# A gated linear recurrence followed by routed experts: a list-scheduled program graph, a one-hot inverse permutation and one evacuation for q and k

## The chip, the cores and the metric

One core of one Trainium2 chip. The time is device microseconds of one execution; a kernel is executed several times and the median is given, with the lowest and highest. Each execution has a state: slow if it took over 1.5% more than the fastest one of the same kernel in the same round of runs, else fast; ratios use fast runs alone. The runs fell on several chips; where a chip is named, it is by the number that the runs record (0, 9 and 15; the chip of the first pair of kernels is not recorded).

Words for the engines: PE is TensorE (PEld its weight loads), DVE is VectorE, ACT is ScalarE, POOL is GpSimd, SP is SyncE, which here only starts transfers.

## The reference

```python
# q, k, v, a_re, a_im: [4, 8, 768, 48];  x: 3072 rows of 384;  8 experts, 384 -> 1024 -> 384
mag = sqrt(a_re**2 + a_im**2); scale = minimum(mag, .999) / (mag + 1e-6)
ar, ai = a_re * scale, a_im * scale
for t in range(768):                                  # per batch and head
    S_re, S_im = ar*S_re - ai*S_im + k[t] v[t]^T, ar*S_im + ai*S_re
    y[t] = q[t] @ S_re
x = rows of y, heads side by side                     # 3072 x 384
for e in range(8):
    m = domain_id == e
    out[m] = relu(x[m] @ w1[e]) @ w2[e]
```

Both kernels run the recurrence in tiles of 256 positions of a batch: 12 tiles ("groups"), each with a preparation (logarithms and angles, running sums by matmul, exponentials, sines) and four **steps**, one per pair of heads: transposes of k and q, scores, a causal mask, outputs. There are 48 steps. The rows of a finished batch are gathered per expert, put through two layers and scattered to the output: 4 x 8 = 32 **expert runs** of 128 rows each.

## The kernel before

Its order is hand-made: `prep` gives eight portions of a group's preparation, spread over the steps of the group before; an expert runs where `plan` says; the weights of expert e are loaded in five parts at steps 1 + 5e on. The inverse permutation (which row goes to which expert slot) is made by 24 scatters to memory and read back:

```python
    def scatter_inverse(b):
        for c in range(6):
            col = b * 6 + c
            unordered(f"inv{b}", nc.gpsimd.indirect_dma_start(
                out=inv_ap[b][:, :],
                out_offset=bass.IndirectOffsetOnAxis(ap=dest_i[:, col:col + 1], axis=0),
                in_=tok_i[:, col // 2, col % 2, :], in_offset=None))

    def load_inverse(b):
        nc.sync.dma_start(out=inv_sb[b][:, :, :], in_=inv_ap[b][0:NMAIN, :].rearrange("(p e) two -> p e two", e=NE))
    # ... in the loop over steps:
            if s == 2:
                for b in range(B):
                    scatter_inverse(b)
                    load_inverse(b)
```

The transposed q and k leave PSUM in two copies, q in turn on ACT and DVE, k always on DVE into a buffer with zeros between its halves:

```python
        if s % 2 == 0:
            nc.scalar.copy(out=qt[...], in_=t_ps[0:96, 0]...)          # cut
        else:
            nc.vector.tensor_copy(out=qt[...], in_=t_ps[0:96, 0]...)   # cut
        nc.vector.tensor_copy(out=kt[...][:, :, 0:3:2, :], in_=t_ps[0:96, 1]...)   # cut
```

The experts' PSUM buffers are one of each kind (`x` for transposes and second layer, `wh` for the first layer), shared with the steps.

Of the kernel before, what the change touches and what calls it, by code (L numbers as in the profile page):

```python
# [29 lines left out]
NE = 8  # L30
# [8 lines left out]
GROUPS = [[0], [1], [2, 3], [4, 5], [6, 7], [8, 9], [10, 11]]  # L39
SET_LE = "natural_log_exp_and_others"  # L40
SET_TRIG = "trig_and_small"


@with_exitstack
def kernel(
# [14 lines left out]

    nosync = mybir.DependencyInfo(mybir.DependencyClass.NoSync, mybir.DependencyReason.DATA)

    def after(ins, prev):
        if prev is not None:
            tc.add_manual_dep(ins.ins, prev.ins.name, nosync, reason="order")
        return ins

    last = {}

    def chain(key, ins):  # L70
        after(ins, last.get(key))
        last[key] = ins
        return ins
# [24 lines left out]
    def src_view(t, g):  # L98
        b, i = divmod(g, NT)
        return t[b, :, i * TS:(i + 1) * TS, :].rearrange("h (p j) d -> p h (j d)", j=2)  # L100

    loaded = {}

    def load(g, names):
        for name, t in names:
            bufs = {"ar": 2, "ai": 2, "q": 2, "k": 2, "v": 2}[name]
            tl = lpool.tile([128, H, 96], F32, name=f"ld_{name}", tag=f"ld_{name}", bufs=bufs)
            nc.sync.dma_start(out=tl[:, :, :], in_=src_view(t, g))
            loaded[name, g] = tl

    ARI = [("ar", a_re), ("ai", a_im)]
    QKV = [("k", k), ("q", q), ("v", v)]
    load(0, ARI)


# [6 lines left out]
    mask = cpool.tile([128, 2, 2, 2, CP], BF16, name="mask")  # L122
    for c in range(2):
        r = slice(c * CP, (c + 1) * CP)
        for js in range(2):
            for jt in range(2):
                u = (u_str if js > jt else u_inc)
                for hh in range(2):
                    nc.vector.tensor_copy(out=mask[r, hh, js, jt, :], in_=u[r, r])
    VB, CB = 2, 2  # L130
    vz = [cpool.tile([128, H, 2, 3, D], BF16, name=f"vz{n}") for n in range(VB)]
    cz = [cpool.tile([96, 2, 2, 3 * CP], BF16, name=f"cz{n}") for n in range(CB)]
# [3 lines left out]
    for t in cz:  # L136
        nc.vector.memset(t[:, :, :, CP:2 * CP], 0.0)
    ident = cpool.tile([128, 128], BF16, name="ident")
    make_identity(nc, ident[:, :])
    ident16 = cpool.tile([128, 128], F16, name="ident16")  # L140
# [8 lines left out]


    dest_i = cpool.tile([128, NCOL], I32, name="dest_i")
    ovf_i = cpool.tile([1, 1], I32, name="ovf_i")
    tok_i = cpool.tile([128, B * NT, 2, 2], I32, name="tok_i")
    inv_sb = [cpool.tile([128, NE, 2], I32, name=f"inv_sb{b}") for b in range(B)]
    XSLOTS = 5
    xrow = [cpool.tile([128, HD], F16, name=f"xrow{n}") for n in range(XSLOTS)]
    for t in xrow:
        nc.gpsimd.memset(t[:, :], 0.0)

    def routing():  # L160
        rpool = mpool
        e8 = rpool.tile([128, 8], F32, name="e8", bufs=1)
        nc.gpsimd.iota(e8[:, :], pattern=[[1, 8]], base=0, channel_multiplier=0,
                       allow_small_or_imprecise_dtypes=True)
        nc.gpsimd.iota(tok_i[:, :, :, 0], pattern=[[TS, B * NT], [1, 2]], base=0, channel_multiplier=2)
        for c in range(2):
            nc.gpsimd.iota(tok_i[c * CP:(c + 1) * CP, :, :, 1].rearrange("p (b i) j -> p b i j", b=B),
                           pattern=[[0, B], [TS, NT], [128, 2]], base=c, channel_multiplier=2)
        sent = rpool.tile([128, NROWS // 64], I32, name="sent", tag="xt", bufs=2)
        nc.gpsimd.iota(sent[:, :], pattern=[[1, NROWS // 64]], base=OOB_SENT, channel_multiplier=NROWS // 64)  # L170
        for b in range(B):
            nc.scalar.dma_start(out=inv_ap[b][:, :].rearrange("(p c) two -> p (c two)", p=128), in_=sent[:, :])

        dom_i = rpool.tile([128, B * NT, 4], I32, name="dom_i", tag="xt", bufs=2)
        h32 = dataclasses.replace(moe_domain_id.tensor, shape=[NTOK * 2], dtype=I32)
        nc.scalar.dma_start(out=dom_i[:, :, :],
                            in_=bass.AP(tensor=h32, offset=0, ap=[[4, 128], [TS * 2, B * NT], [1, 4]]))
        fb = rpool.tile([128, 4, NCOL], F32, name="fb", tag="o_sb", bufs=2)
        rank, main, over = fb[:, 1], fb[:, 2], fb[:, 3]
        domf = fb[:, 0].rearrange("p (c j) -> p c j", j=2)  # L180
        nc.vector.tensor_copy(out=domf[:, :, :], in_=dom_i[:, :, 0:4:2])
        dcol = domf[:, :, :].rearrange("p c j -> p (c j)")
        oh = rpool.tile([128, NCOL, 8], F16, name="oh", tag="xst", bufs=2)
        nc.vector.tensor_tensor(out=oh[:, :, :], in0=e8[:, None, :].to_broadcast([128, NCOL, 8]),
                                in1=dcol[:, :, None].to_broadcast([128, NCOL, 8]), op=ALU.is_equal)
        r_ps = big("r_ps")
        nc.tensor.matmul(out=r_ps[:, 0, 0:NCOL * 8], lhsT=u_str[:, :], rhs=oh[:, :, :], start=True, stop=True)
        nc.tensor.matmul(out=r_ps[:, 1, 0:NCOL * 8], lhsT=ones16[:, :], rhs=oh[:, :, :], start=True, stop=True)
        cr = rpool.tile([128, 2, B, 6, 8], F32, name="cr", tag="h_sb", bufs=2)
        cnt, rk = cr[:, 0], cr[:, 1]  # L190
        nc.vector.tensor_copy(out=cnt[:, :, :, :], in_=r_ps[:, 1, 0:NCOL * 8])
        nc.vector.tensor_copy(out=rk[:, :, :, :], in_=r_ps[:, 0, 0:NCOL * 8])
        for c in range(1, 6):
            nc.vector.tensor_tensor(out=rk[:, :, c, :], in0=rk[:, :, c, :], in1=cnt[:, :, c - 1, :], op=ALU.add)
            nc.vector.tensor_tensor(out=cnt[:, :, c, :], in0=cnt[:, :, c, :], in1=cnt[:, :, c - 1, :], op=ALU.add)
        ovf = rpool.tile([1, 1], F32, name="ovf", bufs=1)
        nc.vector.tensor_reduce(out=ovf[:, :], in_=cnt[0:1, :, 5, :], axis=AX.XY, op=ALU.max)
        nc.vector.tensor_copy(out=ovf_i[:, :], in_=ovf[:, :])
        rk3 = rk[:, :, :, :].rearrange("p b c e -> p (b c) e")
        nc.vector.tensor_tensor(out=rk3, in0=rk3, in1=oh[:, :, :], op=ALU.mult)  # L200
        nc.vector.tensor_reduce(out=rank[:, :], in_=rk3, axis=AX.X, op=ALU.add)
        nc.vector.scalar_tensor_tensor(out=main[:, :], in0=rank[:, :], scalar=float(NE), in1=dcol,
                                       op0=ALU.mult, op1=ALU.add)
        nc.vector.scalar_tensor_tensor(out=over[:, :], in0=dcol, scalar=float(OVC * 128), in1=rank[:, :],
                                       op0=ALU.mult, op1=ALU.add)
        nc.vector.scalar_tensor_tensor(out=over[:, :], in0=over[:, :], scalar=float(NMAIN - CAP), in1=main[:, :],
                                       op0=ALU.add, op1=ALU.subtract)
        nc.vector.tensor_scalar(out=rank[:, :], in0=rank[:, :], scalar1=float(CAP), scalar2=None, op0=ALU.is_ge)
        nc.vector.tensor_tensor(out=over[:, :], in0=over[:, :], in1=rank[:, :], op=ALU.mult)
        nc.vector.tensor_tensor(out=main[:, :], in0=main[:, :], in1=over[:, :], op=ALU.add)  # L210
        nc.vector.tensor_copy(out=dest_i[:, :], in_=main[:, :])

    def scatter_inverse(b):
        for c in range(6):
            col = b * 6 + c
            unordered(f"inv{b}", nc.gpsimd.indirect_dma_start(  # L216
                out=inv_ap[b][:, :],
                out_offset=bass.IndirectOffsetOnAxis(ap=dest_i[:, col:col + 1], axis=0),
                in_=tok_i[:, col // 2, col % 2, :], in_offset=None))

    def load_inverse(b):
        nc.sync.dma_start(out=inv_sb[b][:, :, :], in_=inv_ap[b][0:NMAIN, :].rearrange("(p e) two -> p e two", e=NE))
# [5 lines left out]
    def load_weights(e, part, gate):  # L228
        if part < 3:
            i = nc.gpsimd.dma_start(out=w1t[e][:, part, :], in_=moe_w1[e, part * 128:(part + 1) * 128, :])  # L230
        else:
            j = (part - 3) * 4
            i = nc.gpsimd.dma_start(out=w2t[e][:, j:j + 4, :],
                                    in_=moe_w2[e, j * 128:(j + 4) * 128, :].rearrange("(j p) f -> p j f", p=128))
        tc.add_manual_dep(i.ins, gate.ins.name, syncdep, reason="inputs first")


    lm = {}
    th = {}
    ep = {}  # L240
    em = {}
    sc = {}

    def flat(t):
        return t[:, :, :].rearrange("p h x -> p (h x)")

    def jhd(ap):
        return ap.rearrange("p h (j d) -> p j h d", j=2)

    def hdx(ap):  # L250
        return ap.rearrange("p j (h d) -> p j h d", h=H)
# [384 lines left out]
```

## Time and profile before

| what | before | from |
|---|---|---|
| time, median of the runs with the profile | 355.4 us (349.9 to 355.8) | timed runs |
| span of the profiled execution (taken apart from these four) | 342.6 us | page |
| masks of step 0 / 4 / 26 / 47 | 28.4 / 63.1 / 178.4 / 285.1 us | timeline, `mtm` on DVE |
| expert runs done by step 26 / 47 | 4 / 21 | timeline, `h_sb` |
| last matmul | 331.9 us | timeline |

By the rule above three of these four runs (355.4 to 355.8) count as slow and only 349.9 as fast.

The masks are used as milestones throughout: each step has exactly one. The page's first part gives busy time, share of the span and number of instructions of each engine:

```profile
PE 235.1 (69%) x2642; PEld 178.5 (52%) x2642; DVE 186.3 (54%) x356; ACT 184.0 (54%) x246; POOL 162.2 (47%) x188
```

No engine is near full over the whole span. The slices, the stages and the scatters are shown in the prediction. In the list of waits (total us, times, longest), three of those that end with something the profile calls "remote", that is, a release it can't put to any engine or transfer of this core:

```profile
DVE mtm L405 <- remote: 11.0, 2, 6.1
DVE fg L312 <- remote: 6.9, 1, 6.9
ACT h_sb L462 <- remote: 6.7, 1, 6.7
```

All waits of this kind sum to 38.1 us over the engines (some run at the same time). One of the two on `mtm` and the one on `fg` lie at 37 to 43 and 46 to 53 us.

### The profile page before, as it was taken

The numbers are of one execution on the slowest core, as the hardware profiler recorded it, in microseconds if no ns is written. First come the engines' busy times: TensorE is split into PE (matmuls) and PEld (weight loads), VectorE is DVE, ScalarE is ACT, GpSimd is POOL, SyncE is SP. The second block draws the span as 40 slices with busy tenths as digits, with TensorE's granted clock in tenths as the row PEclk, the third lists the DMA queues.
The fourth block names the chain that finished last, engine by engine and source line by source line (L and its number), as shares of the span: only waits on it lengthen the run. The fifth ranks groups of instructions, "written<-read, shape, count | busy, mean of one in ns | idle before, by whom it ended". The sixth has DMA issues, their size and how long they took to land.

```text
span 342.6 us, 6624 instructions
## 1 busy us (share of the span) xinstructions
PE 235.1 (69%) x2642; PEld 178.5 (52%) x2642; DVE 186.3 (54%) x356; ACT 184.0 (54%) x246; POOL 162.2 (47%) x188
## 2 busy tenths in 40 slices
PE   0247432854567758967685798997899799729960
PEld 0026211731255536755473676785688688527740
DVE  4684236574787659676973878666963241000100
ACT  4545404555287236886593677878563554313540
POOL 5227776162024444453347835535885432752230
PEclk9999555675588679989996999999999999987996
DMA  8970075899929979979979699576547112120110
GB/s 195 234 149 1 7 119 81 186 212 239 274 43 151 232 170 163 189 139 267 246 124 199 165 188 265 140 113 104 121 77 150 59 60 81 57 61 21 54 57 21
DMA packets 83126, 46.40 MB, mean 135 GB/s; under 512 B 68273, under 2 KB 78479, under 8 KB 83088
## 3 DMA queue, kind: packets, MB, share of 16 engines
q1 hardware_dynamic: 64704, 25.99, 32.5%
q0 software_dynamic: 16256, 19.70, 31.6%
q10 hardware_dynamic: 2128, 0.22, 0.5%
q8 instruction: 22, 0.36, 0.5%
q14 instruction: 16, 0.13, 0.2%
HBM read 51.96 MB, written 8.87 MB: 178 GB/s over the span
## 4 chain that ended last, share of the span: by engine, by line
PE 23%; issue 17%; ACT 17%; DVE 13%; DMA 13%; POOL 12%; another core or an unknown queue 1%; POOLq 0%; SPq 0%; DVEq 0%; ACTq 0%
POOL gl_inv_rows L216 6%; PE h_ps L459 5%; PE o_ps L469 5%; PE cum L264 5%; DMA xrow<-gl_x_rows,inv_sb 3%; ACT L479 3%; DMA gl_x_rows<-xst 3%; DMA ld_v<-in_v_dram 3%; POOL out_dram L472 3%; PE t_ps L381 2%; DVE fg L312 2%; PE mt L402 2%; ACT la L272 2%; POOL xrow L441 2%; DMA gl_inv_rows<-tok_i,dest_i 2%
## 5 line engine op out<-in xcount | busy, mean ns | idle before, releaser
L405 DVE TENSOR_TENSOR mtm<-mt,mask 128x512 bf16<-128x512 f32 x48 | 33.0, 687 | 47.9 <-PE mt L402 35.2
L459 PE MATMUL h_ps<-xt,w1t 128*128 128x128 f16 x768 | 51.1, 222 | 6.7 <-ACT h_sb L462 6.7
L472 POOL DMA_INDIRECT out_dram<-o_sb,inv_sb x32 | 33.3, 1040 | 46.9 <-ACT o_sb L471 42.1
L462 ACT ACTIVATE h_sb<-h_ps 128x1024 f16<-128x1024 f32 x32 | 32.7, 1021 | 38.5 <-PE h_ps L459 28.0
L459 PEld LDWEIGHTS <-w1t 128*128 128x128 f16 x768 | 46.6, 100 | 9.3 <-issue 7.6
L469 PE MATMUL o_ps<-w2t,h_sb 128*128 128x384 f16 x256 | 49.5, 336 | 2.1 <-DVE xt L451 1.0
L441 POOL DMA_INDIRECT xrow<-gl_x_rows,inv_sb x32 | 37.1, 1160 | 17.0 <-issue 6.9
L402 PE MATMUL mt<-qt,cz 96*128 96x128 bf16 x384 | 34.2, 237 | 7.7 <-DVE cz L391 6.9
L451 DVE COPY xt<-xt_ps 128x384 f16<-128x384 f16 x32 | 11.3, 352 | 45.0 <-PE xt_ps L449 35.9
L402 PEld LDWEIGHTS <-cz 96*128 96x128 bf16 x384 | 27.4, 107 | 16.0 <-DVE cz L391 10.1
L469 PEld LDWEIGHTS <-h_sb 128*128 128x128 f16 x256 | 24.5, 101 | 16.4 <-issue 3.8
L216 POOL DMA_INDIRECT gl_inv_rows<-tok_i,dest_i x24 | 24.8, 1033 | 16.7 <-DVE fg L315 9.7
L348 POOL CAST vz<-ld_v 64x768 bf16<-64x768 f32 x24 | 24.5, 1020 | 13.3 <-issue 5.1
L421 PE MATMUL y<-vz,mtm 128*128 128x96 bf16 x192 | 20.0, 216 | 15.1 <-DVE mtm L405 9.8
L346 POOL CAST vz<-ld_v 128x768 bf16<-128x768 f32 x12 | 11.8, 980 | 37.1 <-issue 15.4
L318 ACT ACTIVATE sc<-fg 128x768 bf16<-128x768 f32 x12 | 10.1, 843 | 34.0 <-DVE fg L313 24.5
L292 ACT ACTIVATE em<-cum,bias_m 128x768 bf16<-128x768 f32 x12 | 10.8, 897 | 27.1 <-PE cum L264 22.4
L264 PE MATMUL cum<-lm,u_inc 128*128 128x384 f16 x36 | 12.9, 419 | 16.5 <-DVE lm L283 16.5
L230 POOL DMA_DIRECT2D w1t<-in_moe_w_dram x24 | 14.3, 595 | 20.7 <-DVE mtm L405 20.3
L391 DVE COPY cz<-t_ps 96x512 bf16<-96x512 bf16 x48 | 19.8, 412 | 5.8 <-ACT qt L386 4.9
L421 PEld LDWEIGHTS <-mtm 128*128 128x128 bf16 x192 | 13.1, 100 | 18.6 <-DVE mtm L405 12.9
L264 PEld LDWEIGHTS <-ones 128*128 128x128 f16 x96 | 10.3, 116 | 23.5 <-issue 15.6
(90 smaller groups left out, 522.2 us busy)
## 6 DMA issues: line engine op xcount, KB each, us to landing
w1t<-in_moe_w_dram POOLq DMA_DIRECT2D x24, 256.0 KB
w2t<-in_moe_w_dram POOLq DMA_DIRECT2D x16, 384.0 KB
ld_ar<-in_a_re_dram SPq DMA_DIRECT2D x12, 384.0 KB
ld_ai<-in_a_im_dram SPq DMA_DIRECT2D x12, 384.0 KB
ld_k<-in_k_dram SPq DMA_DIRECT2D x12, 384.0 KB
ld_q<-in_q_dram SPq DMA_DIRECT2D x12, 384.0 KB
ld_v<-in_v_dram SPq DMA_DIRECT2D x12, 384.0 KB
gl_x_rows<-xst SPq DMA_DIRECT2D x12, 192.0 KB
```

Of the source, the lines that this page charges most:

```text
L216: unordered(f"inv{b}", nc.gpsimd.indirect_dma_start(out=inv_ap[b][:, :], out_offset=bass.IndirectOffsetOnAxis(ap=dest_i[:, col:col + 1], a ...
L264: chain("pe_cum", nc.tensor.matmul(out=o, lhsT=l[:, :], rhs=r, start=(n == 0), stop=(n == len(mm) - 1)))
L348: nc.gpsimd.tensor_copy(out=vt[c * CP:(c + 1) * CP, :, :, 1 + c, :], in_=vsrc[c * CP:(c + 1) * CP])
L391: nc.vector.tensor_copy(out=kt[:, :, :, :].rearrange("p h j (c t) -> p (h j) c t", c=3)[:, :, 0:3:2, :], in_=t_ps[0:96, 1].rearrange("p h ...
L402: nc.tensor.matmul(out=mt[:, hh, js, :], lhsT=kt[:, hh, js, c * CP:(c + 2) * CP], rhs=qt[:, hh, c, :], start=(c == 0), stop=(c == 1))
L405: m = nc.vector.tensor_tensor(out=mtm[:, :, :, :].rearrange("p a b t -> p (a b t)"), in0=mt[:, :, :, :].rearrange("p a b t -> p (a b t)"), ...
L421: chain("pe_y", nc.tensor.matmul(out=o, lhsT=mtms[s][:, hh, js, :], rhs=vz[g % VB][:, pr * 2 + hh, js, 1:3, :], start=(js == 0), stop=False))
L441: nc.gpsimd.indirect_dma_start(out=x[:, :], out_offset=None, in_=x_ap[b][:, :], in_offset=bass.IndirectOffsetOnAxis(ap=idx, axis=0), bound ...
L459: nc.tensor.matmul(out=h_ps[:, j // 4, (j % 4) * 128:(j % 4 + 1) * 128], lhsT=w1[:, fs, j * 128:(j + 1) * 128], rhs=xt[:, fs, :], start=(f ...
L462: nc.scalar.activation(out=h_sb[:, :, :].rearrange("p j t -> p (j t)"), in_=h_ps[:, :, :].rearrange("p a t -> p (a t)"), func=AF.Relu)
L469: nc.tensor.matmul(out=o_ps[:, :], lhsT=h_sb[:, j, :], rhs=w2[:, j, :], start=(j == 0), stop=(j == 7))
L472: ins = nc.gpsimd.indirect_dma_start(out=out[:, :], out_offset=bass.IndirectOffsetOnAxis(ap=inv, axis=0), in_=o_sb[:, :], in_offset=None, ...
```

## The change

The whole program becomes a graph of some thousand pieces with modelled costs. At build time a list scheduler places each piece, in order of earliest start, on one of the engines allowed for it, and the resulting order is frozen. Beside that: the inverse permutation is computed on chip by one-hot matmuls; k and q leave PSUM in one copy (k transposed with its halves swapped, so that both fit one pattern); the first group is prepared in two halves; value masks are cut from the bf16 tile; weights are spaced for the last part to start at step 26; in the last batch the experts alternate between two PSUM buffers.

```diff
+def order(ops, rings):                       # cut to its core
+    while cand:
+        # for each ready piece: the engine on which it would end first, and its start there
+        t0, e0 = min((x[0], x[1]) for x in best)
+        t, e, c, o = min((x for x in best if x[1] == e0 and x[0] <= t0 + SLACK), key=lambda x: (x[3].pos, x[0]))
+        o.start, o.on = t, e
+        # ... engine, DMA and ring times move on; successors become ready
...
-    def scatter_inverse(b): ...
-    def load_inverse(b): ...
+    def rt_r(b, e):                            # six selections of a batch, on POOL or DVE
+        for c in range(6):
+            (nc.gpsimd if e == "POOL" else nc.vector).tensor_scalar(
+                out=T["R", b][:, c, :], in0=slots[:, :], scalar1=rank[:, b * 6 + c:b * 6 + c + 1], scalar2=None, op0=ALU.is_equal)
+        # ... V = one-hot of the expert times (row, row in batch, 1)
+    def rt_q(b):
+        for c in range(6):
+            nc.tensor.matmul(out=T["I", b][:, :, :], lhsT=T["R", b][:, c, :], rhs=T["V", b][:, c], start=(c == 0), stop=(c == 5))
...
+    def out_kq(s, slot, e):
+        cp(e, kq[slot][:, 0:8 * 3 * CP].rearrange("p (b x) -> p b x", x=3 * CP)[:, :, CP:],
+           tps[s][0:96].rearrange("p k h c t -> p (k h c) t"))
...
+            xr, xi, ti, hi, he, oi, ob = (Inst("xrow"), Inst("tm" if last and e % 2 else "x"), Inst("xt"),
+                                          Inst("cum" if last and e % 2 else "wh"), Inst("h_sb"),
+                                          Inst("tm" if last else "x"), Inst("o_sb"))
```

## The prediction

> **What bounds the kernel now.** I read the page's slices first, then the stages by window, the groups, and the waits.
>
> ```profile
> PE   0247432854567758967685798997899799729960
> DVE  4684236574787659676973878666963241000100
> ACT  4545404555287236886593677878563554313540
> PEclk9999555675588679989996999999999999987996
> DMA  8970075899929979979979699576547112120110
> ```
>
> No engine is full throughout. TensorE (PE) is full only from about slice 25 on; DMA is full from slice 7 to 24; DVE and ACT are half full everywhere. So I cut the span at the masks of steps (48 steps, one `mtm` each; step 0 at 28.4 us, step 4 at 63.1, step 26 at 178.4, step 47 at 285.1):
>
> ```profile
> 0.00:27.30 27.30, 6.57 (x36) 3.53 (x36) 16.89 (x62) 13.31 (x15) 10.18 (x30) 1.00 0.88 181
> 27.30:62.00 34.70, 16.81 (x124) 11.55 (x124) 15.18 (x23) 12.77 (x17) 25.84 (x27) 0.62 0.34 55
> 62.00:116.60 54.60, 34.11 (x295) 23.14 (x296) 38.30 (x57) 30.04 (x40) 15.75 (x20) 0.69 0.95 190
> 116.60:200.00 83.40, 62.83 (x720) 47.80 (x718) 60.02 (x103) 55.88 (x75) 42.10 (x44) 0.89 0.92 191
> 200.00:289.00 89.00, 81.12 (x1123) 67.35 (x1122) 52.65 (x102) 56.29 (x81) 48.16 (x48) 1.00 0.57 119
> 289.00:333.50 44.50, 33.61 (x351) 25.09 (x348) 3.22 (x9) 15.67 (x22) 19.86 (x20) 0.92 0.17 56
> ```
>
> Columns: length, then busy PE, weight loads, DVE, ACT, POOL, then PE clock, DMA share, GB/s. Five regimes: a serial prologue; 34.7 us in which only POOL works (25.84) and DMA falls to 0.34; 138 us with DMA at 0.92 to 0.95 and DVE and ACT near 70%; 89 us with PE at 81.12 of 89; a tail with PE at 75%.
>
> Why the second stage is empty is in the waits of the SP queue:
>
> ```profile
> SPq L222 <- DMA gl_inv_rows<-tok_i,dest_i: 32.1, 5, 12.2
> ```
>
> (in total, times, longest), and in the groups (busy, mean ns, then idle before with its releasers):
>
> ```profile
> L216 POOL DMA_INDIRECT gl_inv_rows<-tok_i,dest_i x24 | 24.8, 1033 | 16.7 <-DVE fg L315 9.7
> L391 DVE COPY cz<-t_ps 96x512 bf16<-96x512 bf16 x48 | 19.8, 412 | 5.8 <-ACT qt L386 4.9
> L386 ACT COPY qt<-t_ps 96x512 bf16<-96x512 bf16 x24 | 13.9, 578 | 6.2 <-PE t_ps L381 5.9
> L348 POOL CAST vz<-ld_v 64x768 bf16<-64x768 f32 x24 | 24.5, 1020 | 13.3 <-issue 5.1
> L469 PE MATMUL o_ps<-w2t,h_sb 128*128 128x384 f16 x256 | 49.5, 336 | 2.1 <-DVE xt L451 1.0 <-ACT o_sb L471 0.6 <-ACT h_sb L462 0.5
> ```
>
> The 24 scatters of the inverse permutation hold POOL from 23.0 to 56.0 us, and the SP queue, in order, holds the next groups' loads behind reading that inverse back. The chain of waits goes through exactly this (scatters, then a read-back landing, then `ld_v` from 61.7 for 6.6 us).
>
> **What the Trainium skill says.** "VectorE: DVE Perf Modes", section "Why PSUM operands drop a tier": a PSUM operand allows at most the packed 16-bit mode. The trace agrees: 512 bf16 elements in 412 ns is 267 ns of streaming at two per cycle of 0.96 GHz plus 145 fixed. "PSUM — Partial Sum Buffer", section "The four PSUM rules": POOL cannot touch PSUM; so freed POOL time can only take SBUF pieces (here `values`, `vmask`, selections), none of the evacuations. "DMA: Bandwidth & Descriptors", Specifications: transfers under 512 B are below line rate; 68273 of the 83126 packets are that small, and a 0.95 share moves only 190 GB/s. "TensorE: Matmul & The Clock Gate", Part 1: an idle window of about 3.4 us halves the clock; the trace agrees: after 5.4 us idle at 301 us, one expert's first layer took 2.72 us instead of 1.50.
>
> **The change part by part.**
> - Inverse permutation. Removed: 24 scatters x 1.033 = 24.8 us of POOL, four fills, four read-backs, and 20-odd small DVE operations. Added: per batch seven small selection operations on DVE or POOL, six small matmuls, three small DVE operations: some 2 us a batch (an estimate from the 0.17 to 0.36 us of the small routing operations). None of it is needed before step 12. What it frees is the second stage. The next group's preparation is seven ACT operations of 0.84 to 0.93, two exponentials of 0.9 and two table loads of 1.28, 10.4 us, with some 10 us of DVE interleaved; so step 4 can come 16 to 18 us after step 0 rather than 34.7: about -17 us.
> - First group in two halves, routing behind it. Now DVE does routing while `em` and `th` wait (13.1 to 21.9 us), and ACT and DVE alternate on full tiles. Halves pipeline, at more fixed cost: about -5 us.
> - One evacuation for q and k. 1024 elements by the rate above: 533 + 145 = 0.68 us on DVE, 48 x 0.68 = 32.6 us. It replaces 48 x 0.412 + 24 x 0.412 on DVE (29.7) and 13.9 on ACT. Sum -11 us of engine time, and one semaphore hop less per step; the 6.9 us that scores waited for `cz` are all the path can gain from that.
> - Value masks from the bf16 tile, on DVE or POOL. POOL's 24.5 us of 64-row casts become about 0.72 us per group on DVE (12 groups, 8.6 us, an estimate from a 768-element cast at the fastest mode plus fixed time) or twice the POOL time of now. POOL was no bound after 62 us, so this is near zero.
> - Placement by earliest finish. DVE + ACT now total 186 + 184 = 370 us; the change leaves about 367. Both can be near 184, while PE needs, at full clock from the chain's pieces, 48 steps x 1.26 (0.45 scores, 0.45 transposes, 0.36 outputs), 12 x 1.05 state, 32 of running sums (192 matmuls of 384 columns at 0.165, six in 0.99) and 32 experts x 2.81 (1.34 + 1.30 + 0.17): 60 + 13 + 32 + 90 = 195 us. DMA's two big queues take 32.5% + 31.6% of 342.6 = 220 us. Four resources near 190 to 220 us: the end is set by how well they overlap.
> - Weights earlier: the last part at step 26 instead of 40. By step 26 DMA did 0.88x27.3 + 0.34x34.7 + 0.95x54.6 + 0.92x61.8 = 145 us of work; 14 more weight parts of about 1.75 us (an estimate: 70 us of the 108 on the software queue over 40 parts) make 168.
> - Tail: hidden and output PSUM tiles alternate between two buffers for the last batch. An expert now takes 3.07 us (each `out_dram` 3.07 apart, 312.7 to 328.0) and can take PE's 2.81: 8 x 0.26 = 2 us. Experts of batch 2 filling the wait of about 5.4 us from the last x store to the first gathered row (289.2 to 294.6): about 4 us more.
>
> **The sum.** Step 0 at 22, step 4 at 39. Step 26: from the engines (DVE + ACT, about 113 us each by then, at 75% use) 150; from DMA, 168/0.95 = 177. I take 165, since no engine waits for loads for long in 62 to 200 now (`vz` waited 13.6 us for `ld_v`, most of it at the start) and weights may land late. After it: 22 steps at 1.95 us of PE (running sums and states included) is 43, and 25 experts x 2.81 is 70: 113 us, against 78% use before (331.9 - 178.4 = 153 us for 120); I give the new order 93%: 121 us. Then 10.7 from the last matmul to the end, as now (331.9 to 342.6). 165 + 121 + 11 = 297 for a profiled execution. The timed median lies 3.7% above the profile now (355.4 against 342.6), some of it luck in the stalls: four stalls of 4.8 to 6.9 us (38 to 43, 47 to 53, 263 to 268, 301 to 306) where engines wait for something the profile calls remote or issue. I add 1%: **300 us**.
>
> **Rivals.**
> 1. DMA takes the place of the scatters. For it: share 0.95 already, and the change asks for 25 us more by step 26. Single-buffered q, k, v loads leave less slack. Then step 26 stays at 177 or later, and the end is 310 to 330.
> 2. The list order is frozen from modelled costs. Queues are strictly in order, so a piece whose inputs are late blocks those behind it; waits move from PE to elsewhere. For it: clocks of 0.62 to 0.69 early, which a fixed matmul cost ignores, and stalls of 5 us. Against: the order now is hand-made and frozen too, at 78%. If use stays near 80%, the end is 318.
> 3. Everything overlaps as planned: DMA's 220 us less the tail's share packed before the last 35 us gives a floor near 255; 270 to 280 if engines hold 90% from the start.
> 4. Nothing or worse, if a new queue (POOL with gathers behind weight gates) blocks the experts: needs all of 55 us to be eaten; unlikely.
>
> **Range and chances.** 276 (rival 3) to 330 (1 and 2 together, plus stalls). Faster than 348 us needs only the second stage's 17 us and something of the rest: 0.92. Within 2%: 0.05. Slower: 0.03.
>
> **What would show it.** Right: no scatters or read-back; step 0 near 22 and step 4 near 39 us; a single evacuation of 96x1024 near 0.68 us; DVE and ACT each near 184 us; PE above 90% after step 26; last experts 2.8 us apart. Wrong: DMA share under 0.85 between steps 4 and 26 with engines still idle (the order, not DMA, is the bound), long waits of POOL for masks with PE idle behind gathers, or PE waiting on evacuations after step 26.

## The result, and the profile after

The changed kernel takes **307.5 us** (305.1 to 310.5), the kernel before 355.4 in the same runs: ratio 0.872, 95% interval 0.857 to 0.887. A ratio here is the mean time of one kernel's fast runs over that of the other's of the same rounds, profiled executions left out, so not quite the ratio of the medians quoted. This first one can't be recomputed exactly from the runs listed: 306.7 over the one fast run of 349.9 would be 0.877. The profiled execution took 310.5 us and counts as slow; the kernel was profiled again later in a fast execution (span 305.3), whose milestones are the same within 3.5 us.

The slices of the changed kernel (span 308.7 us, a slice is 7.7 us):

```profile
PE   1335738457687899167498689899889999877960
DVE  4969878858999897047979669897579444100100
ACT  3667578838869984027697549675765344434430
PEclk9999988956999999769799879999999999999997
DMA  7998599999999999978989523517321021112110
```

DVE is fuller in the first half than before (8 and 9 where 5 to 7 stood), the hollow of the scatters is gone from all lines, and DMA is done with its bulk at slice 22 rather than 31. The same as stages, cut at the masks and where the picture changes (columns: length; busy PE, weight loads, DVE, ACT, POOL; PE clock, DMA share, GB/s):

```profile
0.00:32.80 32.80, 11.47 (x117) 8.90 (x118) 24.76 (x89) 19.06 (x30) 15.81 (x41) 1.00 0.95 205
32.80:49.20 16.40, 10.36 (x115) 8.03 (x115) 13.16 (x23) 13.03 (x15) 3.94 (x6) 0.90 0.97 178
94.30:111.00 16.70, 14.26 (x197) 11.61 (x198) 15.07 (x27) 14.99 (x20) 11.84 (x14) 1.00 1.19 253
111.00:133.00 22.00, 13.02 (x191) 11.01 (x189) 11.13 (x18) 7.58 (x12) 9.19 (x11) 0.86 1.13 234
200.00:258.90 58.90, 55.48 (x760) 45.57 (x759) 41.18 (x72) 32.72 (x44) 22.25 (x21) 1.00 0.27 76
258.90:300.00 41.10, 33.87 (x402) 25.75 (x399) 3.69 (x11) 17.36 (x24) 19.40 (x20) 1.00 0.18 57
```

Row 1 is the prologue: it got longer, 32.8 us. Row 2: the first four steps take 16.4 us instead of 34.7. Rows 3 and 4: the DMA share is over 1, and in row 4 the engines are half idle all the same. Row 5: PE at 94%.

| milestone | before | predicted | after |
|---|---|---|---|
| step 0 | 28.4 | 22 | 32.8 |
| step 4 | 63.1 | 39 | 49.2 |
| step 26 | 178.4 | 165 | 163.6 |
| step 47 | 285.1 | | 258.2 |
| last matmul | 331.9 | 286 | 298.9 |
| span | 342.6 | 297 | 308.7 |

The total came out 2.5% above the predicted 300. On the way three stretches were off by over 10 us, not all in one direction (to step 0, steps 4 to 26, and after step 26), so the experiments go at the parts.

Two views bear on the prologue, and a third is used later. First, the chain of waits from 7 to 19 us (start, length, what), in which two blocks of selections on POOL stand in the path:

```profile
8.62 0.36 DVE rank L479
...
9.08 4.79 POOL sel L484 x6
...
13.92 0.21 PE iv_ps L493
...
14.29 4.00 POOL sel L484 x6
```

Then the durations of the selections by engine, from the answer for the tile `sel` (minimum/median/maximum in ns, first and last start in us):

```profile
L484 POOL TENSOR_SCALAR sel<-slots,rank x12: 598/712/1101, 9.1 to 17.6; 128x128 f16<-128x128 f16 x12
L484 DVE TENSOR_SCALAR sel<-slots,rank x12: 240/259/376, 10.7 to 16.5; 128x128 f16<-128x128 f16 x12
```

and, for later, of the value masks, from that for `vz`, where 64 rows are copied bf16 to bf16:

```profile
L643 DVE COPY vz<-vz x20: 340/357/534, 12.8 to 236.6; 64x768 bf16<-64x768 bf16 x20
...
L643 POOL COPY vz<-vz x4: 1028/1037/1149, 24.1 to 153.7; 64x768 bf16<-64x768 bf16 x4
```

The routing of all four batches, which nothing needs before step 12, runs at 9 to 19 us, because the scheduler takes whatever can start. Its model has 2.2 us for a batch's selections on POOL; they took 4.79 and 4.00. The routing's matmuls (`iv_ps`) waited 4.3 us for POOL in eight places, and the running sums of group 0 stand behind them in PE's queue: in the chain, the next of them starts at 19.91, after the routing's last piece. POOL's slowness is not the whole of it: with all selections on DVE (fixed engines, below) step 0 still comes at 32.9 us. Nor is it enough that the selections stand in the prologue: in the kernels of experiments 1 and 3 they ran there too, between 12 and 27 us among DVE's other work, and step 0 came at 28.7 and 27.6. What differs is, likely, the place that the list gave them before other work.

### The profile page after: what moved, and what is told of

It reads as the page before. It is cut to its first block, busy times and chain, and to the rows that moved or that the text cites. A ratio compares the mean times of both kernels' runs of the same rounds, so it can differ in the third digit from the quotient of the medians.

```text
span 308.7 us, 6669 instructions
## 1 busy us (share of the span) xinstructions
PE 221.2 (72%) x2699; PEld 172.1 (56%) x2699; DVE 199.5 (65%) x372; ACT 183.2 (59%) x239; POOL 122.8 (40%) x154
## 2 busy tenths in 40 slices
DMA packets 81238, 46.16 MB, mean 150 GB/s; under 512 B 66385, under 2 KB 76591, under 8 KB 81200
## 3 DMA queue, kind: packets, MB, share of 16 engines
q0 software_dynamic: 15488, 19.68, 32.9%
## 4 chain that ended last, share of the span: by engine, by line
PE 34%; DVE 18%; issue 12%; DMA 11%; POOL 11%; ACT 10%; SPq 1%; POOLq 0%; DVEq 0%; ACTq 0%
PE h_ps L760 8%; PE cum L583 7%; DMA ld_k<-in_k_dram 7%; PE o_ps L777 6%; PE t_ps L686 4%; POOL out_dram L786 4%; POOL xrow L740 3%; POOL sel L484 3%; PE mt L704 3%; DMA ld_ar<-in_a_re_dram 2%; PE w_ps L666 2%; DVE kcat L637 2%; DVE kq L643 2%; DVE ld_ar L614 2%; PE y L722 2%
## 5 line engine op out<-in xcount | busy, mean ns | idle before, releaser
L786 POOL DMA_INDIRECT out_dram<-o_sb,inv_sb x32 | 36.5, 1142 | 66.6 <-ACT o_sb L642 55.1
L643 DVE COPY kq<-t_ps 96x1024 bf16<-96x1024 bf16 x40 | 27.1, 683 | 16.0 <-PE y L727 10.9
L704 PE MATMUL mt<-kq 96*128 96x128 bf16 x384 | 30.5, 224 | 4.0 <-DVE kq L643 2.1
L686 PE MATMUL t_ps<-swap,kcat 128*96 128x128 bf16 x192 | 20.5, 234 | 12.3 <-DVE kq L643 11.7
L704 PEld LDWEIGHTS <-kq 96*128 96x128 bf16 x384 | 23.8, 100 | 7.3 <-DVE kq L643 3.2
L588 ACT ACTIVATE em<-cum,bias_m 128x768 bf16<-128x768 f32 (+1 forms) x13 | 11.1, 850 | 26.1 <-PE cum L583 26.1
L666 PE MATMUL w_ps<-vz,kcat 128*96 128x96 bf16 x192 | 14.6, 229 | 15.1 <-DVE kcat L637 8.9
L686 PEld LDWEIGHTS <-kcat 128*96 128x96 bf16 x192 | 16.1, 135 | 13.2 <-issue 12.8
L666 PEld LDWEIGHTS <-kcat 128*96 128x96 bf16 x192 | 13.1, 143 | 18.3 <-DVE kcat L637 10.5
L686 PE MATMUL t_ps<-ident,qcat 128*96 128x128 bf16 x192 | 20.3, 233 | 0.9 <-DVE qcat L637 0.9
L642 ACT COPY o_sb<-o_ps 128x384 f32<-128x384 f32 x26 | 12.4, 479 | 14.3 <-PE o_ps L777 10.4
```

Of the source, the lines that this page charges most:

```text
L643: nc.gpsimd.tensor_copy(out=out, in_=in_) if e == "POOL" else nc.vector.tensor_copy(out=out, in_=in_))
L666: nc.tensor.matmul(out=o[:, :, h], lhsT=cat["k", g][:, j, hq * 4 + h].rearrange("p a d -> p (a d)"), rhs=vz[g % VB][:, hq * 4 + h, j, 0:2, ...
L686: nc.tensor.matmul(out=o, lhsT=cat[name, g][:, j, pr * 2 + hh].rearrange("p a d -> p (a d)"), rhs=(swap if kind == 0 else ident)[:, :], is ...
L704: nc.tensor.matmul(out=mt[:, hh, js, :], lhsT=kts[s][:, base + (1 - c) * 2 * CP:base + (2 - c) * 2 * CP], rhs=block(s, 4 + 2 * hh + c), st ...
L786: ins = nc.gpsimd.indirect_dma_start(out=out[:, :], out_offset=bass.IndirectOffsetOnAxis(ap=inv, axis=0), in_=o_sb[:, :], in_offset=None, ...
```

## Experiments

Twelve kernels, each timed in three rounds beside the kernel before. "Fixed engines" is the changed kernel with every piece allowed on one engine only; it serves as base for later edits because its times spread less (302.9 to 304.2).

The first four ran on chip 0. There the kernel before had fast runs of 348.5 to 350.3 us, three of 355.7 to 358.3 counted slow, and one stray of 480.5.

**1. The kernel before with the one-hot inverse alone.**

```diff
-                for b in range(B):
-                    scatter_inverse(b)
-                    load_inverse(b)
+            if s in (2, 4, 6, 8):
+                inverse(s // 2 - 1)     # selections on DVE, six matmuls, as in the change
```

> The kernel before with only the inverse permutation changed (one-hot matmuls, selection on DVE, one batch each at steps 2, 4, 6 and 8; four gather slots instead of five, for space). If the 24 scatters and the read-back behind them held the second stage, step 4 comes at 44 to 48 us instead of 63.1 and the time falls by 12 to 20 us, to 335 to 343. Rival: the preparation of group 1 on ACT and DVE would have held that stage anyway; then step 4 stays after 55 us and the time falls by less than 7.

Measured: 331.6 us (331.0 to 333.7), ratio 0.951 (0.941 to 0.962); step 4 at 50.6 us instead of 63.1 (44 to 48 expected), step 26 at 163.8 instead of 178.4. That is 17 us, the size that the prediction gave this part. The written order of everything else was left alone; the ranks come from matmuls too, and there are four gather slots in place of five. The selections are written at steps 2 to 8, but in the trace they run at 12.8 to 25.3 us, before step 0.

**2. The kernel before with one evacuation alone.**

```diff
-        if s % 2 == 0:
-            nc.scalar.copy(out=qt..., in_=t_ps...)
-        else:
-            nc.vector.tensor_copy(out=qt..., in_=t_ps...)
-        nc.vector.tensor_copy(out=kt..., in_=t_ps...)
+        nc.vector.tensor_copy(out=kts[s][:, 0:8 * 3 * CP].rearrange("p (b x) -> p b x", x=3 * CP)[:, :, CP:],
+                              in_=t_ps[0:96].rearrange("p k h c t -> p (k h c) t"))
```

> The kernel before with only the evacuation of q and k changed (one 96x1024 copy on DVE, emitted after the outputs of the step before, because two slots fit and not three; four gather slots). If the evacuation was on the path only for the 6.9 us that scores waited, the time moves by 0 to -7 us (348 to 355). Rival: DVE now carries all of it, nothing on ACT, and the group preparations on DVE come later: up to +6 us.

The copy is also emitted after the outputs of the step before, and there are four gather slots. Measured: 344.6 us (344.5 to 345.8), ratio 0.987 (0.980 to 0.995), some 4 us. The scatters are still there, and the first mask behind them waited 14.2 us in the profile, so step 4 even came at 69.8.

**3. Both.**

> The kernel before with both. If the two parts are independent, the sum of their gains, about -17 to -22 us (333 to 338), and the rest of the measured 48 us (26 to 31) belongs to order, placement, earlier weights and the tail. Rival: the parts overlap with each other and the sum is not reached by more than 5 us.

Measured: 320.7 us (320.1 to 322.0), ratio 0.917 (0.911 to 0.923): 29 us, against 17 + 4 for the parts. After the inverse, the one evacuation is worth 11 us (331.6 to 320.7), more than the 6.9 that the prediction allowed it. Both expectations fall: the sum of the parts is exceeded. About two thirds of the whole gain of some 43 us need no scheduler.

**4. The change with every piece on one engine.**

```diff
-        r = op("rt_r", {"DVE": 1.0, "POOL": 2.2}, ...)
+        r = op("rt_r", {"DVE": 1.0}, ...)
-            ok = op("out_kq", {"DVE": .69, "ACT": 1.06}, ...)
+            ok = op("out_kq", {"DVE": .69}, ...)
# and so on: wraps on DVE; values and value masks on POOL; state, x rows, hidden and expert outputs on ACT; xt on DVE
```

> The changed kernel, its list scheduler kept, but every piece allowed on one engine only: evacuations of q and k, wraps and xt on DVE, hidden, output, x and state on ACT, values, masks of values on POOL. If the choice of engine is what makes the order overlap, it costs 8 to 15 us (315 to 322). Rival: loads bound the time up to step 26 and PE after it, so the choice is worth less than 2% (304 to 313).

Measured: 303.2 us (302.9 to 304.2), ratio 0.868 (0.862 to 0.873). My theory falls, the rival holds: the choice of engine brings nothing (the list order changes with it, so the two were not parted).

The next four ran on chip 9. There the kernel before took **333.9 us** (332.3 to 334.7) in all seven runs, 16 us less than the fast runs on chip 0. Times of different rounds can therefore not be compared directly; milestones of the same instruction stream up to step 47 can (experiment 7 has the same order as experiment 4 up to the tail, and its marks agree within 3 us).

**5. Half the weights (wrong).** The other half of the experts use the first four's weights.

```diff
-        "weights": lambda o, e, p, s: weights(e, p, s),
+        "weights": lambda o, e, p, s: weights(e, p, s) if e < 4 else None,
-        ... ffn_h, X["te", b, e], w1t[e], ...       and w2t[e]
+        ... ffn_h, X["te", b, e], w1t[e % 4], ...   and w2t[e % 4]
```

> Wrong on purpose: from the changed kernel with fixed engines (303.2 us, order unchanged), the weights of experts 4 to 7 aren't loaded and the weights of 0 to 3 are used in their place; same instructions on all engines else, 4 x 8.75 = 35 us of DMA work less before step 26. Theory (the stretch of steps 4 to 26 is held by the DMA engines, whose mean busy share there was over 1.1): step 26 comes 15 to 30 us earlier than 159.8 and the whole 8 to 20 us earlier, 283 to 295 us, the rest given back to the experts, which come to stand behind. Rival (the in-order queues hold that stretch and the DMA engines have slack): step 26 within 5 us, whole 299 to 304 us.

Measured: 299.2 us (298.4 to 300.2), step 26 at 154.9, against 159.2 with all weights on the same chip (experiment 7). The rival holds: from 111 us on, where the weights of experts 4 to 7 would have come, the DMA share is roughly halved, and PE is hardly faster. Its weak point is that it takes nothing away before step 12; experiment 12 mends that.

**6. Late routing.** The selections of batch b may not start before a given mask.

```diff
+RT = (6, 10, 14, 18)
+    for b in range(B):
+        sels[b].deps.append(MK[RT[b]])      # sels: the pieces rt_r; MK: the masks
```

> From the changed kernel with fixed engines: each batch's selections and one-hot matmuls may not start before the mask of step 6, 10, 14, 18, which puts the routing behind the prologue as the prediction had it. Theory (the routing that the list schedule put into the prologue made step 0 late; it is 32.9 us where 22 was predicted): step 0 at 25 to 28 us and step 4 at 43 to 46, but since the DMA engines hold the next stretch, step 26 only 0 to 4 us earlier and the whole 0 to 4 us faster than 303.2: 299 to 303. Rival (the prologue is on the path to the end): the whole 5 to 7 us faster, 296 to 298. Second rival: the routing costs the same wherever it stands, no change or slower by up to 3 us.

Measured: **290.5 us** (289.1 to 292.7), ratio 0.873 (0.867 to 0.878) to a kernel before that itself takes only 333.9 there. Step 0 comes at 27.4 us, step 4 at 47.0, step 47 at 242.6, where the base's stream on the same chip has 32.8, 50.5 and 248.4. The stages of this kernel:

```profile
0.00:27.40 27.40, 8.29 (x85) 6.59 (x86) 18.12 (x61) 16.54 (x26) 11.55 (x32) 1.00 1.07 232
...
157.70:242.60 84.90, 78.96 (x1098) 65.68 (x1097) 63.49 (x105) 53.42 (x73) 46.31 (x42) 1.00 0.44 111
242.60:278.30 35.70, 33.56 (x406) 25.92 (x403) 3.99 (x12) 16.60 (x23) 18.70 (x19) 1.00 0.21 66
```

Step 47 gains 5.8 us, about the 5.4 that step 0 gains, so the prologue is likely on the path to the end. My theory (hidden behind DMA) falls. The gain isn't simply carried through, though: steps 16 and 20 come later than in the base (114.6 and 128.3 against 109.6 and 125.9), and the list order that follows is a different one; PE is 93% busy after step 26.

**7. Ordinary PSUM buffers in the tail.**

```diff
-Inst("tm" if last and e % 2 else "x") ... Inst("cum" if last and e % 2 else "wh") ... Inst("tm" if last else "x")
+Inst("x") ... Inst("wh") ... Inst("x")
```

> From the changed kernel with fixed engines: the experts of the last batch use the ordinary PSUM buffers (x, wh) instead of alternating with those of the steps that are done. Theory (the alternation is what makes the tail after step 47 4 to 6 us shorter than that of before with the two other changes, 51.0 against 56.5): last mask unchanged within 2 us, tail 55 to 58 us, whole 306 to 309 us. Rival (the tail is held by gathers and by the matmuls themselves, about 2.8 us per expert): 302 to 305 us.

Measured: 302.5 us (300.7 to 305.2); from step 47 to the end 50.6 us. Inconclusive: the base has 51.0 and 49.1 us there on chips 0 and 15, but with remote stops of 5 us inside (two and one), which no profile on chip 9 has; on chip 9 kernels with the alternation have 45.5 (experiment 6) and 49.6 (experiment 5). The theory's 55 to 58 us fall, and the rival's 302 to 305 hold by the number. Up to the last matmul, though, the two with the alternation on chip 9 take 35.7 us from step 47 and this one 40.8. So the alternation may be worth 1 to 5 us, and it was not separated from the rest.

**8. Experiment 3 with the weights as early as in the change.**

```diff
-    w_slot = {e: 1 + 5 * e for e in range(NE)}
+    w_slot = {e: int(.65 + .65 * (5 * e + 4)) - 4 for e in range(NE)}   # and the parts at .65 + .65 (5e + n)
```

> From the kernel before with the one-hot inverse and the one evacuation (320.7 us), alone the weights are loaded as early as in the change (five parts of an expert in 3.25 steps in place of 5) and each expert may start as early as its weights allow by the same rule as before. Theory (some 8 of the 17 us between that kernel and the changed one come from experts that can run earlier): 7 experts done by step 26 or 36 in place of 4 and 12 by 36 at least, step 47 later by 0 to 3 us, tail shorter, whole 311 to 316 us. Rival (earlier weights only crowd the loads of the steps, and the order is what matters): 318 to 325 us.

Measured: 321.9 us (320.4 to 323.8), ratio 0.964 (0.958 to 0.970). Seven experts have reached their hidden layer by step 26 (six have ended it), as hoped, and that at 162.6 us, where experiment 3 has four by 161.6; but what was saved is lost again after it. The rest, step 26 to the last matmul:

```profile
162.60:311.80 149.20, 123.54 (x1532) 100.14 (x1530) 70.96 (x119) 75.08 (x102) 66.32 (x65) 0.90 0.35 89
```

Three experts fewer remain than in experiment 3, and it takes 149 us with PE at 83%; experiment 3 itself takes 148.9 and its repetition 145.5 (on other chips, at clocks of 0.97 and 0.98 rather than 0.90). The rival holds by its number: early weights alone, in the hand-made order, show no gain. Experiment 3 was not run on this chip, so a loss isn't excluded.

The last four ran on chip 15, where the kernel before took 349.8 us (347.4 to 351.0).

**9. The changed kernel again.**

> The changed kernel once more, because the kernel before took 355 us in the first two rounds of runs and 334 us on the chip of the third. Theory (the stops of about 5 us that the first traces show belong to those chips and cost the kernel before some 20 us, the changed one 5): on a chip where before takes 334 the change takes 300 to 304, a ratio near 0.90; where before takes 355 it takes 305 to 310, a ratio near 0.87. Rival (the whole chip is faster by 6%): 287 to 292 us where before takes 334.

Measured: 306.2 us (304.0 to 307.1), ratio 0.874 (0.868 to 0.879). Before takes neither of the two times foreseen; the ratio is that of the first runs.

**10. Fixed engines again.**

> The changed kernel with each piece on one engine, again, as the base for half weights, late routing and ordinary tail buffers, which ran on another chip than its first run. Theory (choice of engine brings nothing): within 2% of the changed kernel, 298 to 303 us where before takes 334, and then the tail buffers are worth under 3 us, half the weights under 4 and the late routing about 10. Rival (the choice is worth something on this chip): over 306 us.

Measured: 301.2 us (300.4 to 301.9), ratio 0.862 (0.857 to 0.867). Beside experiment 9 on the same chip it is 1.6% faster, with no overlap of the runs.

**11. Experiment 3 again.**

> The kernel before with the one-hot inverse and the one evacuation, again, as the base for the early weights. Theory from its first trace (15 us of stops in 320 us): where before takes 334 us it takes 306 to 312 us, so that earlier weights (321.9) made it slower by some 12 us and the list order has only 5 to 10 us left to it. Rival (no such stops in it): 318 to 322 us, and the early weights change nothing.

Measured: 319.2 us (317.8 to 321.1), ratio 0.912 (0.907 to 0.916), as on chip 0 and as the rival has it; but the rival's ground (no stops) is not there, since its remote waits sum to 12.2 us. Whether it would be 10 us faster on chip 9 stays open. Within this call: before 349.8, both 319.2, fixed engines 301.2, the change 306.2.

**12. One expert's weights (wrong).** As experiment 5, but all experts use expert 0's.

```diff
-        ... weights(e, p, s) if e < 4 else None      w1t[e % 4]   w2t[e % 4]
+        ... weights(e, p, s) if e < 1 else None      w1t[0]       w2t[0]
```

> Wrong on purpose: as half weights, but only expert 0's weights are loaded and all experts use them, 7 x 8.75 = 61 us of DMA work less before step 26, 15 of the 20 parts that are issued before step 12 among them. Theory (after half weights moved step 26 by only 5 us, the in-order queues with DVE at over 80% hold steps 4 to 26, not the DMA engines): step 12 within 4 us of the 92.5 of fixed engines, step 26 at 150 to 156, the whole 295 to 301. Rival (the DMA engines hold the steps up to 12, where half weights took nothing away): step 12 at 78 to 86, the whole 284 to 293.

Measured: 305.6 us (301.1 to 308.7; two of the four runs count as slow, the fast ones are 301.1 and 304.0), no faster than the 301.2 with all weights; profiled span 299.1, as that one's. Step 12 at 89.2 instead of 91.8, step 26 at 153.4 instead of 158.9, step 47 at 246.0 instead of 250.0, last matmul 3.0 us earlier. The stages of steps 4 to 12 and 12 to 26, with all weights (experiment 10):

```profile
50.20:91.80 41.60, 26.78 (x281) 18.81 (x280) 34.23 (x49) 28.46 (x37) 13.82 (x18) 0.84 1.05 199
91.80:158.90 67.10, 55.41 (x698) 43.29 (x697) 54.28 (x83) 43.84 (x58) 42.01 (x46) 0.92 1.15 241
```

and with one expert's:

```profile
49.50:89.20 39.70, 24.77 (x279) 17.95 (x278) 34.42 (x48) 27.84 (x35) 7.08 (x7) 0.91 0.50 123
89.20:153.40 64.20, 51.73 (x698) 41.70 (x697) 54.60 (x83) 43.92 (x59) 31.55 (x28) 1.00 0.63 152
```

The DMA share (second number from the right) falls from 1.05 to 0.50 and from 1.15 to 0.63, and the stages shorten by 1.9 and 2.9 us. The whole stretch is thus held by the volume of loads for at most some 5 us of 109. With all weights one load does stand in the chain of waits, `ld_k` for 22.8 us from 125.07 on; with one expert's no load does, and no more than that is gained. In the prologue and the first four steps the share did not change (0.94 and 0.89 with all weights, 0.93 and 0.96 with one expert's), so nothing is shown for them. DVE is over 80% busy in both stages and has the same busy time in both kernels; that the rest is queues waiting for one another was not shown.

## Why the prediction was right, and where its steps were not

The time, the sign and the largest part were right: 307.5 measured for 300 predicted, inside the range of 276 to 330. The closeness of the total is in part luck: in the profile, step 0 comes 10.8 us late, steps 4 to 26 take 11.6 less and the work after step 26 takes 14.3 more than predicted, and these add up to most of the 11.7 by which the span misses 297. Step by step:

- **Scatters removed, -17 us: right** (experiment 1, 17 us at the end, 12.5 of them by step 4). With a reservation: my "only POOL works" overstates (the row itself has PE at 16.8 and DVE at 15.2 us), and of the 34.7 us that the first four steps took before, 13 are two stops of DVE with a remote release (6.1 and 6.9 us, the waits shown above). In the kernels without the scatters the first such stop comes after 200 us. The kernel before is 16 us faster on chip 9. Those stops may be the reason, but no profile of it was taken there, so it is argued, not shown. What the scatters cost on chip 9 was not measured; fixed engines with ordinary tail buffers gain 31 us there in all (experiment 7).
- **First group in halves with the routing behind it, -5 us and step 0 at 22: wrong by 10.8 us.** This is the term that failed. I took "routing behind" from the intent; the list scheduler knows no behind, only a start time, and put the routing of all batches into the prologue. Experiment 6 shows that holding it back brings step 0 to 27.4 and step 47 forward by 5.8 us. The 5 us of the halves show nowhere: experiment 3, with the first group whole and the selections still in the prologue, has step 0 at 27.6. The halves were never tried alone, so why none of it shows stays open.
- **Step 4 sixteen to eighteen us after step 0: right**, 16.4 us.
- **One evacuation, 0.68 us on DVE and at most 6.9 us: duration right, value too small by the timed runs.** The group's row after (busy us, mean ns of one, then idle time before):

```profile
L643 DVE COPY kq<-t_ps 96x1024 bf16<-96x1024 bf16 x40 | 27.1, 683 | 16.0 <-PE y L727 10.9
```

  683 ns against 0.68 worked out. It is worth 4 us while the scatters hold the start and 11 us after (experiments 1 to 3). The difference lies at the start: from step 4 to step 47 it saves 6.8 us in the one profile (222.0 to 215.2) and 6.4 in the other (222.4 to 216.0), near the 6.9 allowed; up to step 4 it loses 6.7 in the one (with the stop of 14.2 us) and gains 2.9 in the other. As stops of `mtm` with a remote release (4.8 and 6.1 us) lie in the stretch of the two profiles without the one evacuation, how much of the 6.8 and 6.4 is the evacuation stays open.
- **Value masks, near zero: the durations were right** (two copies of 0.357 on DVE, 0.71 us per group against an estimated 0.72). Their value was not tried alone.
- **Placement by earliest finish, DVE and ACT each near 184 us: wrong for DVE, harmless.** After, DVE has 199.5 and ACT 183.2 us; 40 of 48 evacuations went to DVE. Fixing the engines is 1.6% faster on the same chip, so no gain of this half of the idea shows; what is left of the change after experiment 3 is order, weights, halves of the first group, value masks and tail buffers, together 18 us (319.2 to 301.2 on one chip). Weights alone bring nothing (8), tail buffers at most 5 us (7), so most of it may be the order, which was never run alone: argued, not shown. PE was put at 195 us at full clock and shows 221.2 busy at a mean granted clock of 0.93; at that clock 195 would be 210.
- **Step 26 at 165: right at 163.6, by two errors.** It starts 10 us late (step 4 at 49.2 instead of 39) and steps 4 to 26 take 114.4 us instead of 126. I had stretched that part toward a DMA bound of 168 us of work (its terms, 145 + 14 x 1.75, give 169) at a share of at most 0.95. The work was right: the shares times the lengths up to 163.6 us sum to 170. The ceiling was wrong: the share reaches 1.19. And it is hardly a bound: with 35 of 40 weight parts, some 61 us of that work by the prediction's 1.75 us each, taken away, step 26 comes 5.5 us earlier and the end not at all (experiment 12). Rival 1 is refuted, for fixed engines by experiment and for the change by step 26 itself. Row 4 of the stages after (111 to 133 us, engines half idle) has a load of k in the chain:

```profile
111.05 20.73 DMA ld_k<-in_k_dram
```

  Fixed engines, with the same volume, have no such hollow there (PE 19.9 of the same 22 us). They wait for a load of k later, 22.8 us from 125.07 on with PE busy for 16.8 of 23 us, and reach step 26 only 3.7 us earlier than the change (both on chip 15: 158.9 and 162.6). In the changed kernel itself no load was taken away.
- **After step 26, 113 us of PE at 93%, 121 us: too short by 14.** From the mask of step 26 to the last matmul, before, after and with late routing:

```profile
178.40:331.90 153.50, 129.31 (x1622) 103.46 (x1620) 69.64 (x133) 84.55 (x118) 81.09 (x81) 0.96 0.50 112
```

```profile
163.60:298.90 135.30, 118.42 (x1502) 93.57 (x1500) 74.09 (x127) 74.00 (x97) 56.21 (x53) 0.97 0.32 85
```

```profile
157.70:278.30 120.60, 112.52 (x1502) 91.61 (x1500) 67.49 (x116) 70.03 (x96) 65.01 (x61) 1.00 0.37 98
```

  PE is busy 118.4 us, 88% of 135.3 (84% before; my 78% put 120 us where the row shows 129.3). Of the 14.3 us over the prediction, 5.4 are PE work beyond its 113 and 8.9 are idle time beyond the 8 it allowed. With late routing PE is busy 112.5 of 120.6 us, 93%: close to the sum predicted, but for another order, and on a chip without stops. Of the 14.7 us between these two, 5.9 are PE busy for longer with the same 1502 matmuls (mean granted clock 0.97 against 1.00) and 8.8 are idle time. Four of the 8.8 lie in steps 28 to 32 (the change, then late routing) and four in the tail, where the change has a remote stop of 5.2 us:

```profile
168.80:200.30 31.50, 25.54 (x293) 19.36 (x293) 24.38 (x39) 19.97 (x26) 12.05 (x12) 0.89 0.46 123
```

```profile
162.30:181.60 19.30, 17.34 (x233) 14.05 (x233) 17.54 (x29) 15.36 (x21) 11.54 (x12) 1.00 0.81 186
```

  Two thirds of what makes this stretch longer in the change is work that it does there (PE 25.5 against 17.3 us). The longest POOL wait in it (total, times, longest) is a gather whose row buffer is free only when PE has transposed the rows in it,

```profile
POOL xrow L740 <- PE xt_ps L748: 11.1, 1, 11.1
```

  but this gather is not in the chain of waits. What the chain has of POOL comes just before and at the start of the stretch, here from POOL's timeline (start, length, what, idle time before it and its releaser):

```profile
164.59 0.78 POOL L514 DMA_DIRECT2D w2t<-in_moe_w_dram  x1 [1.68 <-DVE mtm L709]
165.68 1.04 POOL L740 DMA_INDIRECT xrow<-gl_x_rows,inv_sb  x1 [0.30 <-issue]
167.03 2.21 POOL L740 DMA_INDIRECT xrow<-gl_x_rows,inv_sb  x1 [0.30 <-issue]
169.54 1.00 POOL L740 DMA_INDIRECT xrow<-gl_x_rows,inv_sb  x1 [0.30 <-issue]
170.58 0.82 POOL L643 CAST vz<-ld_v 128x768 bf16<-128x768 f32 x1
```

  A weight part waits for the mask of step 26, three gathers stand behind it, and behind these the value cast that the next outputs need. That is the prediction's fourth rival, in small: a queue that blocks what the steps need. It was read from the chain and not tried by an experiment, and what it costs stays open. So rival 2 (the frozen order costs waits) is the one that seems partly true.
- **Tail, 2 + 4 us shorter: right in sum.** Step 47 to the last matmul takes 46.8 us before and 40.7 after, with eleven expert runs left in both. But the sign "last experts 2.8 us apart" fails: the stores of the last eight come 3.1 us apart on average (2.9 before), so the gain lies before them, the first of the eight being stored 19.7 us after step 47 and not 27.6. The sum came out right by errors that cancel. How much of it is buffers and how much remote stops (6.7 us on `h_sb` in the one, 5.2 in the other) was not separated.

## What to carry to other kernels

A list scheduler takes what can start, so work that nobody needs yet should be given an earliest time, or it may be put before work on which the start waits; here that was worth 5.4 us at step 0. Try the simple parts of a large change alone in the old order first: here two of them brought 29 of some 43 us. And before a full-looking DMA line is called a bound, take its load away: a share over 1 that was halved moved step 26 by 5.5 us and the end by nothing.

Two variants beat both kernels: fixed engines (301.2 against 306.2 us for the change on one chip), and with late routing besides 290.5 us, 13% below the kernel before on its chip. The change itself was not run on that chip; fixed engines with ordinary tail buffers took 302.5 us there.

## What the Trainium skill lacked or had wrong

- "GPSIMD Engine Reference", section "Engine selection", has one-input work on POOL as roughly line rate. Here a 128x128 comparison with a scalar per partition took 712 ns on POOL and 259 on DVE (medians), and a 64x768 bf16 copy 1037 and 357: 2.7 and 2.9 times.
- "DMA: Bandwidth & Descriptors", section "Specifications", gives the size below which packets lose line rate, but not that packet times summed can exceed the span. With 66385 of 81238 packets under 512 B, the share (packet times over the span of 16 engines) reached 1.19 at 253 GB/s, so packet times overlap, and 1.0 is no ceiling.
- No page that I found has the stops with a remote release: mostly 4 to 7 us at a time, 14.2 once, 38.1 us summed over the engines in the kernel before, 5.7 and 12.6 in two profiles of the change, none in four kernels on chip 9. The kernel before took 334 us there and 347 to 358 on the other two numbered chips (one stray run aside). What they are, these runs don't tell.
